# Converting float64 weights with 16-bit operations into a word of their own, in an attention and two-layer feed-forward kernel

## Chip, cores and metric

One NeuronCore of a Trainium2 chip runs the kernel. The metric is the device time of one execution in microseconds; the time before is the median of three runs.

## What is computed

The inputs are attention operands in float32 and the weights of two gated feed-forward layers in float64. Shapes: batch 4, 8 heads, 576 positions, head width 64; 2304 tokens of width 512; hidden width 1536.

```python
scores = q @ k.T / sqrt(64) + (cum[:, None] - cum[None, :])   # cum = cumsum(log(clip(f)))
attn   = softmax(causal(scores)) @ v                          # per batch and head
x      = attn as [2304, 512]
xn     = x / sqrt(mean(x*x) + 1e-6) * rms_g
y      = (silu(xn @ w_gate) * (xn @ w_val)) @ w_out           # first layer
z      = (silu(y @ w2_gate) * (y @ w2_val)) @ w2_out          # second layer, the output
```

Matrix products keep near-float32 accuracy: each operand is split into a rounded high part and a remainder, and three products of parts (high·high, high·low, low·high) are added up in PSUM.

## The kernel before

**Tokens and groups.** The tokens are worked on in four groups: three of 512 and a last one of 768. For each group the attention of its tokens comes first, then the norm, then the two layers. Attention work of a later group is put between the matmuls of an earlier one.

**Weights.** A layer has 36 weight tiles of 128 x 512 (24 for the gate and value products, 12 for the output product), so a group uses 72. The float64 values come from HBM only once, for group 0: `convert(i)` turns tile i into float32, stores it in HBM (`w_f`), and `split` makes the high and low parts (`whl`: a copy at L301, a subtraction at L306). Groups 1 and later fetch the float32 tiles or the split ones from HBM and convert nothing. In groups 0 to 2 one tile feeds four steps (`mm3`, L1700 to L1702) of three 512-column matmuls, so four L1702 matmuls stand for one tile used.

**Conversion.** One float64 is two 32-bit words. The tile lands in `x` (named `w`, from `w64_slots`: 4 buffers, one of them lent out at the start). Five operations follow:

- L1632 to L1636, the rebase: the high word, read as float32, times 2^-112, into `t`. On ACT (L1632), DVE (L1634) or POOL (L1636).
- L1642 (ACT) or L1644 (DVE), the low word's top three bits: byte 3 of each value is shifted right by 5 and written over byte 4, the lowest byte of the high word, in place. It has to wait for the rebase, which reads that word.
- L1648 (DVE): the high word with all but the sign and those three bits masked off, into `k` (`wk`, 2 buffers). After it `x` is free, and the load of a later tile (L1623) can be issued.
- L1654 (DVE): `t` shifted left by 3, joined with `k`. The result is the float32 tile.
- then the store (L1658) and `split`.

**Order of the work.** A planner written in Python runs when the program is built. Every operation is a request with one or more engines, a duration in us for each, and sometimes a handicap in us that is added to the end of that choice. The planner always takes the request that can start earliest by its model, ties going by priority, and puts it at the end of the chosen engine's queue. What it writes is a fixed order for each in-order engine; on the chip the engines wait by semaphores only. `DVL` stands for DVE operations that it doesn't let run beside a POOL operation. The handicaps are lists by phase (`HAND_LOW[plan.phase]`): phase 0 lasts until group 0 has used eight tiles, phase 1 until group 1 has, and so on. While group 0 has not used twelve tiles, the planner fills gaps of TensorE with matmuls whose result nobody uses (L372; L381 at the very start).

**Where the conversion meets other work.** In group 0 DVE and ACT also do the softmax (L672, L680, L700), the norm (sums at L966 to L972, a power on POOL at L1003, three small copies at L1008, the scaled rows at L1025, split into `X` at L301 and L306) and the gate (L1794, L1796, L1817).

Of the kernel before, what the change touches and what calls it, by code (L numbers as in the profile page):

```python
# [8 lines left out]
F32 = mybir.dt.float32  # L9
F32R = mybir.dt.float32r  # L10
I32 = mybir.dt.int32
U8 = mybir.dt.uint8
AF = mybir.ActivationFunctionType
ALU = mybir.AluOpType
AX = mybir.AxisListType
# [75 lines left out]
SP_START, SP_GATE = 1.55, 3  # L91
# [180 lines left out]
def tile_attention_moe_moe(  # L272
# [1334 lines left out]
    users = [1 + (i // FIRST == 1) for i in range(TOTAL)]  # L1607
    last_use = [0.0] * TOTAL

    def split(i, t, e):  # L1610
# [8 lines left out]
    def convert(i):  # L1619
        x, e0 = yield Take(w64_slots, (w_raw[i - 1],) * (i > 0) + (cum_here,) * (i == W_FREE))  # L1620
        later(w_raw[i], e0)
        src = (w1, w2)[i // NPIECE][i % NPIECE].bitcast(I32)
        el = yield op("SP", dma(P * WP * 8), lambda: nc.sync.dma_start(x.rearrange("p n t -> p (n t)"), src), e0)  # L1623
        t, e1 = yield Take(w32_slots, (el, w_t32[i - 1]) if i else (el,))
        later(w_t32[i], e1)
        k, e2 = yield Take(wk_slots, ())
        u8 = x.rearrange("p n t -> p (n t)").bitcast(U8).rearrange("p (n t) -> p n t", t=8)
        high = x[:, :, 1]

        et = yield either(  # L1630
            (("ACT", act(WP) + 0.06, 0.0), ("DVL", dve2(WP), HAND_CONV[plan.phase]), ("POOL", 0.7, HAND_CONV[plan.phase])),
            lambda e: nc.scalar.mul(t, high.bitcast(F32), 2.0**-112)  # L1632
            if e == "ACT"
            else nc.vector.tensor_scalar(t, high.bitcast(F32), 2.0**-112, None, op0=ALU.mult)  # L1634
            if e == "DVE"
            else nc.gpsimd.tensor_scalar(t, high.bitcast(F32), rebase, 1.0, op0=ALU.mult, op1=ALU.mult),  # L1636
            el, e1,
        )
# [12 lines left out]
        ti = t.bitcast(I32)  # L1651
        e = yield op(
            "DVL", dve(WP) + 0.035,
            lambda: nc.vector.scalar_tensor_tensor(ti, ti, 3, k, op0=ALU.logical_shift_left, op1=ALU.bitwise_or), e, et,  # L1654
        )
        wk_slots.give(k, e)
        later(w_split[i], e)
        es = yield op("SP", dma(P * WP * 4), lambda: nc.sync.dma_start(w_d[i], t), e)  # L1658
        later(stored[i], es)
        e = yield from split(i, t, e)  # L1660
        w32_slots.give(t, Event(max(e.t, es.t)))
# [32 lines left out]
            yield wait(w_raw[i])  # L1694


    def mm3(o, w, c, x, start, stop):
        (xh, xl), cs = (t[:, :NW] for t in x), slice(c * P, (c + 1) * P)
# [12 lines left out]
    def moe():  # L1711

        n = NW
        for g in range(NG):
            at = 0
            ready = [[x_ready[g][i][k] for i in range(2)] for k in range(KT)]
            for layer in range(2):
                base = (2 * g + layer) * NPIECE
                h_ready = [Event() for _ in range(MT)]
                if g == NG - 1:  # L1720
                    yield wait(w_raw[base - 1])
                    for r in range(MT // 2):
# [18 lines left out]
                for m in range(MT):  # L1741
                    pair = []
                    for j in range(2):
                        pc = base + 2 * m + j
                        bank, e0 = yield Take(banks, (w_ready[pc], *ready[0]))
                        for k in range(KT):
                            e = yield op(
                                "PE", 3 * pe(n),
                                lambda: mm3(bank, w_tiles[pc], k, XX[k], k == 0, k == KT - 1),
                                e0, w_ready[pc], *ready[k],  # L1750
                            )
                        used(pc, e)
                        later(steps[g][at], e)
                        at += 1
                        pair.append((bank, e))
                        if j == 0:
                            mid = Event()
                            half = []
                            spawn(gate(bank, e, half, mid), 0.0)
                        else:  # L1760
                            spawn(finish(pair, half, mid, HH[m], h_ready[m], H_PSUM[g](2 * m)), 0.0)
                    progress(g, at)
                if layer:
                    later(x_free[g + 1], e)
                y_ready = [Event() for _ in range(KT)]
                for d in range(KT):
                    bank, e0 = yield Take(banks, (h_ready[0],))
                    for j in range(3):
                        pc = base + 2 * MT + 3 * d + j
                        for c in range(4):  # L1770
                            m = 4 * j + c
                            e = yield op(
                                "PE", 3 * pe(n),
                                lambda: mm3(bank, w_tiles[pc], c, HH[m], m == 0, m == MT - 1),
                                e0, w_ready[pc], h_ready[m],
                            )
                        used(pc, e)
                        later(steps[g][at], e)
                        at += 1
                    spawn(evac(bank, e, layer, d, g, y_ready[d]), 0.1)  # L1780
                    progress(g, at)
                ready = [[y] for y in y_ready]
            if g == NG - 2:
                later(h_free, e)

    def progress(g, at):
# [4 lines left out]
    def gate(bank, e, half, mid):  # L1791
        n = NW
        th, e0 = yield Take(tmp_slots, ())
        e = yield op("ACT", actp(n), lambda: nc.scalar.activation(th, bank, AF.Tanh, scale=0.5), e, e0)  # L1794
        e = yield op(
            "DVE", dve(n), lambda: nc.vector.scalar_tensor_tensor(th, th, 1.0, bank, op0=ALU.add, op1=ALU.mult), e,  # L1796
        )
        banks.give(bank, e)
        half.append(th)
# [6 lines left out]
        half.append(th)  # L1806
        later(mid, e)

    def finish(pair, half, mid, hl, ready, psum):
        n = NW  # L1810
        bank, e = pair[1]
        yield wait(mid, e)
        th = half[0]
        hi, lo = hl
        o = bank if psum else th
        e = yield op(
            "DVE", dve(n), lambda: nc.vector.scalar_tensor_tensor(o, th, 0.5, bank, op0=ALU.mult, op1=ALU.mult), e, mid,  # L1817
        )
        if psum:
            tmp_slots.give(th, e)  # L1820
# [88 lines left out]
```

## Time and profile before

| | |
|---|---|
| runs | 1101.67, 1098.95, 1102.04 us; median 1101.67 us |
| the profiled execution | 1098.85 us, its span 1097.1 us (1.75 us lie around the span) |
| mean granted TensorE clock | 0.989 |
| busy in the span | PE 1078.0 us (98%), DVE 803.8 (73%), ACT 628.6 (57%), POOL 468.2 (43%) |
| moved by DMA | 282.21 MB, 257 GB/s in the mean |

PE is TensorE, PEld its weight load, DVE VectorE, ACT ScalarE, POOL GpSimd, SP SyncE, which issues the DMAs. Times in rows are us from the span's start, unless marked ns. A granted clock of 1.0 is 2.4 GHz, 0.5 is 1.2 GHz. "x41" counts instructions. Rows of one in-order engine can overlap a little: a row's duration runs from start to end, and the next one may start before that end. PE's busy time counts the unused fill matmuls too.

### The profile page before, as it was taken

Reading aid. Unit: us, or ns where it says so; the run is one execution under the profiler, and the core shown is the slowest. Engines: PE = TensorE matmul, PEld = TensorE weight load, DVE = VectorE, ACT = ScalarE, POOL = GpSimd, SP = SyncE. Lnnn points to the kernel's source line nnn. Section 1 sums busy time; section 2 is a strip of 40 time slices with the busy share of each in tenths; the row PEclk is TensorE's granted clock in tenths of the full one; section 3 lists DMA queues with packets and bytes.
Section 4 is the critical chain, followed back from the end, with each engine's and each line's share of the span. In section 5 each row is a group of like instructions: output and inputs, shape, how many; then the busy total and the mean of one; then the engine's idle time right before and its main releaser. Section 6 shows DMA issues by size and latency. Waiting matters only on the chain.

```text
span 1097.1 us, 17688 instructions
## 1 busy us (share of the span) xinstructions
PE 1078.0 (98%) x5547; PEld 949.6 (87%) x5547; DVE 803.8 (73%) x1709; ACT 628.6 (57%) x1409; POOL 468.2 (43%) x492
## 2 busy tenths in 40 slices
PE   8989999998999999999999999999999999999998
PEld 7968888886888888888888888888889999999998
DVE  5989888889556655866756776777767878788773
ACT  4967787886555765677525565456643334443352
POOL 2323211334156665666515585558732441233410
PEclk8989999998999999999999999999999999999999
DMA  7746679664799776776699999997996557754683
GB/s 211 221 160 223 226 262 317 223 228 142 267 383 374 255 247 234 251 251 237 242 345 377 332 341 346 355 343 276 336 332 203 168 188 243 240 171 173 198 261 106
DMA packets 136496, 282.21 MB, mean 257 GB/s; under 512 B 14674, under 2 KB 57490, under 8 KB 136402
## 3 DMA queue, kind: packets, MB, share of 16 engines
q1 hardware_dynamic: 136404, 281.10, 74.6%
q8 instruction: 44, 0.72, 0.3%
q14 instruction: 48, 0.39, 0.1%
HBM read 194.32 MB, written 86.65 MB: 256 GB/s over the span
## 4 chain that ended last, share of the span: by engine, by line
PE 90%; DVE 5%; DMA 2%; POOL 1%; issue 1%; ACT 0%; SPq 0%; POOLq 0%; ACTq 0%
PE bank L1700 18%; PE bank L1702 17%; PE bank L1701 17%; PE bank L1414 5%; PE bank L1416 5%; PE bank L1415 5%; PE bank L939 3%; PE bank L911 3%; PE bank L1324 3%; PE bank L1323 3%; PE bank L1322 3%; PE bank L802 2%; PE bank L803 2%; DMA w<-w 1%; PE bank L658 1%; PE bank L734 1%
## 5 line engine op out<-in xcount | busy, mean ns | idle before, releaser
L306 POOL TENSOR_TENSOR whl<-w,whl 128x512 fp32r<-128x512 f32 x126 | 167.2, 1330 | 216.9 <-ACT whl L301 178.2
L1700 PE MATMUL bank<-X,whl 128*128 128x512 f32 x564 | 227.5, 403 | 3.3 <-ACT X L301 3.3
L1702 PE MATMUL bank<-X,whl 128*128 128x512 f32 x564 | 221.0, 392 | 0.0
L1701 PE MATMUL bank<-X,whl 128*128 128x512 f32 x564 | 221.0, 392 | 0.0
L301 ACT CAST whl<-w 128x512 fp32r<-128x512 f32 x179 | 110.7, 622 | 47.8 <-PE bank L1701 17.7
L1700 PEld LDWEIGHTS bank<-X,whl 128*128 128x128 f32 x564 | 106.6, 189 | 23.8 <-ACT X L301 3.5
L1702 PEld LDWEIGHTS bank<-X,whl 128*128 128x128 f32 x564 | 106.3, 189 | 23.1
L1701 PEld LDWEIGHTS bank<-X,whl 128*128 128x128 f32 x564 | 106.6, 189 | 19.6 <-DVE X L306 0.4
L1700 PE MATMUL bank<-H,whl 128*128 128x512 f32 x215 | 87.4, 407 | 4.4 <-ACT whl L301 4.4
L1702 PE MATMUL bank<-H,whl 128*128 128x512 f32 x215 | 85.4, 397 | 0.2 <-DVE whl L306 0.2
L1701 PE MATMUL bank<-H,whl 128*128 128x512 f32 x215 | 85.2, 396 | 0.0
L1804 ACT ACTIVATE tmp<-bank 128x384 f32<-128x384 f32 x48 | 23.6, 491 | 90.8 <-DVE bank L1452 90.5
L1636 POOL TENSOR_SCALAR w<-w,rebase 128x512 f32<-128x512 f32 x24 | 24.8, 1038 | 106.1 <-PE bank L1702 42.2
L1794 ACT ACTIVATE tmp<-bank 128x512 f32<-128x512 f32 x72 | 43.3, 601 | 40.6 <-PE bank L1702 39.1
L1796 DVE SCALAR_TENSOR_TENSOR tmp<-tmp,bank 128x512 f32<-128x512 f32 x72 | 49.2, 684 | 22.7 <-ACT tmp L1794 22.0
L306 DVE TENSOR_TENSOR whl<-w,whl 128x512 fp32r<-128x512 f32 x71 | 49.5, 702 | 20.9 <-ACT whl L301 20.6
L820 DVE TENSOR_REDUCE tm<-bank 128x1 f32<-128x512 f32 (+1 forms) x96 | 50.4, 561 | 17.9 <-PE bank L803 9.1
L1817 DVE SCALAR_TENSOR_TENSOR bank<-tmp,bank 128x512 f32<-128x512 f32 x60 | 41.6, 694 | 26.6 <-PE bank L1702 25.9
L1642 ACT ACTIVATE w<-w,kbias 128x512 uint8<-128x512 uint8 x41 | 60.2, 1468 | 1.1 <-DVE w L1634 0.6
L923 DVE TENSOR_TENSOR pl<-bank,ph 128x512 fp32r<-128x512 f32 (+1 forms) x80 | 49.9, 632 | 11.3 <-ACT ph L301 10.5
L306 POOL TENSOR_TENSOR kb<-raw,k 64x576 fp32r<-64x576 f32 x31 | 44.3, 1429 | 20.2 <-ACT k L301 14.2
L1700 PEld LDWEIGHTS bank<-H,whl 128*128 128x128 f32 x215 | 40.6, 189 | 13.5 <-ACT whl L301 4.9
(296 smaller groups left out, 2900.4 us busy)
## 6 DMA issues: line engine op xcount, KB each, us to landing
whl<-w_split SPq DMA_DIRECT2D x90, 512.0 KB
w<-w SPq DMA_DIRECT2D x72, 512.0 KB
w<-w_f SPq DMA_DIRECT2D x144, 256.0 KB
w_split<-whl SPq DMA_DIRECT2D x72, 512.0 KB
w_f<-w SPq DMA_DIRECT2D x72, 256.0 KB
w_sums<-w SPq DMA_DIRECT2D x48, 256.0 KB
w_sums_split<-whl SPq DMA_DIRECT2D x23, 512.0 KB
w<-w_sums SPq DMA_DIRECT2D x41, 256.0 KB
```

Of the source, the lines that this page charges most:

```text
L301: nc.scalar.copy(o, i)
L306: (nc.vector if e == "DVE" else nc.gpsimd).tensor_tensor(o, a, b, op=ALU.subtract)
L820: em = yield op("DVE", dve(m), lambda: nc.vector.tensor_reduce(st[:, c + i : c + i + 1], bank[:, :m], axis=AX.X, op=ALU.max), e)
L923: e = yield op("DVE", dve(n), lambda: nc.vector.tensor_tensor(low, src, o.bitcast(F32), op=ALU.subtract), e)
L1414: nc.tensor.matmul(o, w[:, 0, cs], xh, start=c == 0, stop=False)
L1415: nc.tensor.matmul(o, w[:, 0, cs], xl, start=False, stop=False)
L1416: nc.tensor.matmul(o, w[:, 1, cs], xh, start=False, stop=c == 1)
L1642: lambda e: nc.scalar.activation(u8[:, :, 4], u8[:, :, 3], AF.Identity, scale=1.0 / 32, bias=kbias)
L1700: nc.tensor.matmul(o, wh[:, cs], xh, start=start, stop=False)
L1701: nc.tensor.matmul(o, wh[:, cs], xl, start=False, stop=False)
L1702: nc.tensor.matmul(o, wl[:, cs], xh, start=False, stop=stop)
L1796: "DVE", dve(n), lambda: nc.vector.scalar_tensor_tensor(th, th, 1.0, bank, op0=ALU.add, op1=ALU.mult), e,
```

## The change

The two operations on the high word in place give way to two that write 16-bit halves of `k`: the low word's top 16 bits shifted right by 13 go to the lower half of `k` (ACT or DVE), and the high word's top 16 bits, masked to the sign, go to its upper half (DVE). Neither touches `x`, so neither waits for the rebase any more; both wait for the load and for a free `k`. L1654 waits for all three. On ACT the shift is a scale of 1/8192 with a bias that makes rounding act as a floor. In the planner the durations become 0.65 us (ACT) and 0.447 us (DVE) for the low half, 0.447 us for the sign, and the rebase on POOL is put at 1.04 us in place of 0.7. `HAND_LOW` becomes 0.5 in phases 0 and 1 (before: -0.22 and 0).

The diff also brings a way of running the first hidden tiles of group 0 in halves (`halves`, `SPLIT_M`); `SPLIT_M` is 0, so none of it runs, and `mm3`, `gate` and `finish` get arguments that leave their instructions as they were.

```diff
-HAND_LOW = (-0.22, 0, 9, -0.01, 0.08)
+HAND_LOW = (0.5, 0.5, 9, -0.01, 0.08)
+A16, D16, S16 = 0.65, 0.447, 0.447
+SPLIT_M = 0
...
-    nc.gpsimd.memset(kbias, -15.5 / 32)
+    nc.gpsimd.memset(kbias, -4095.5 / 8192)
...
-        u8 = x.rearrange("p n t -> p (n t)").bitcast(U8).rearrange("p (n t) -> p n t", t=8)
+        x16 = x.rearrange("p n t -> p (n t)").bitcast(U16).rearrange("p (n t) -> p n t", t=4)
+        k16 = k.bitcast(U16).rearrange("p (n t) -> p n t", t=2)
...
-            (("ACT", act(WP) + 0.06, 0.0), ("DVL", dve2(WP), HAND_CONV[plan.phase]), ("POOL", 0.7, HAND_CONV[plan.phase])),
+            (("ACT", act(WP) + 0.06, 0.0), ("DVL", dve2(WP), HAND_CONV[plan.phase]), ("POOL", 1.04, HAND_CONV[plan.phase])),
...
-        e = yield either(
-            (("ACT", 1.465, 0.0), ("DVL", 0.762, HAND_LOW[plan.phase])),
-            lambda e: nc.scalar.activation(u8[:, :, 4], u8[:, :, 3], AF.Identity, scale=1.0 / 32, bias=kbias)
+        ek = yield either(
+            (("ACT", A16, 0.0), ("DVL", D16, HAND_LOW[plan.phase])),
+            lambda e: nc.scalar.activation(k16[:, :, 0], x16[:, :, 1], AF.Identity, scale=1.0 / 8192, bias=kbias)
             if e == "ACT"
-            else nc.vector.tensor_scalar(u8[:, :, 4], u8[:, :, 3], 5, None, op0=ALU.logical_shift_right),
-            et,
+            else nc.vector.tensor_scalar(k16[:, :, 0], x16[:, :, 1], 13, None, op0=ALU.logical_shift_right),
+            el, e2,
         )
-        e = yield op(
-            "DVL", dve2(WP), lambda: nc.vector.tensor_scalar(k, high, 7 - 2**31, None, op0=ALU.bitwise_and), e, e2
-        )
+        e = yield op("DVL", S16, lambda: nc.vector.tensor_scalar(k16[:, :, 1], x16[:, :, 3], 2**15, None, op0=ALU.bitwise_and), el, e2)
+        e = both(e, ek)
         w64_slots.give(x, Event(max(e.t, et.t)))
```

## Rows read from the trace of the kernel before

**Rows 1.** The page's 40 slices of the span: PE's busy tenths.

```profile
PE   8989999998999999999999999999999999999998
```

**Rows 2.** Stages of group 0 by windows: length, then busy us (instructions) of each engine, clock, DMA.

```profile
0.00:71.00 71.00, 60.73 (x377) 56.14 (x377) 57.22 (x174) 47.50 (x157) 21.15 (x30) 0.92 0.70 216
71.00:190.00 119.00, 118.92 (x537) 97.94 (x537) 102.28 (x199) 93.33 (x162) 21.77 (x18) 0.98 0.72 240
190.00:264.00 74.00, 74.00 (x347) 61.60 (x346) 63.22 (x124) 58.66 (x112) 25.58 (x23) 1.00 0.62 209
...
24.00:62.00 38.00, 37.56 (x265) 34.99 (x263) 36.49 (x114) 33.73 (x115) 12.42 (x11) 1.00 0.73 236
```

**Rows 3.** Waits of PE in 0 to 300 us: total, times, longest.

```profile
PE bank L1700 <- ACT X L301: 3.3, 1, 3.3
```

**Rows 4.** Timeline of PE around 264 us: start, duration, instruction.

```profile
263.78 0.40 PE L1701 MATMUL bank<-H,whl 128*128 128x512 f32 x1
264.01 0.40 PE L1702 MATMUL bank<-H,whl 128*128 128x512 f32 x1
268.82 0.79 PE L1700 MATMUL bank<-H,whl 128*128 128x512 f32 x1 [4.42 <-ACT whl L301]
...
274.36 0.40 PE L1700 MATMUL bank<-H,whl 128*128 128x512 f32 x1
```

**Rows 5.** Windows, the L1654 joins of DVE alone: length, busy us (instructions), clock, DMA.

```profile
0.00:71.00 71.00, 6.03 (x9) 0.92 0.70 216
71.00:190.00 119.00, 24.77 (x35) 0.98 0.72 240
190.00:264.00 74.00, 13.60 (x18) 1.00 0.62 209
```

**Rows 6.** Windows, the L1702 matmuls alone: PE busy, weight load busy.

```profile
71.00:190.00 119.00, 60.34 (x152) 28.97 (x152) 0.98 0.72 240
190.00:264.00 74.00, 37.12 (x95) 18.03 (x96) 1.00 0.62 209
```

**Rows 7.** Timeline of DVE, 257 to 267 us.

```profile
257.45 0.51 DVE L1008 COPY sm<-sm 32x8 f32<-32x8 f32 x3
...
261.68 5.31 DVE L1025 SCALAR_TENSOR_TENSOR tmp<-xT,gam,mb 128x256 f32<-128x256 f32 x6
266.91 1.21 DVE L1654 SCALAR_TENSOR_TENSOR w<-w,wk 128x512 int32<-128x512 int32 x1
```

**Rows 8.** Timeline of POOL at 261 us.

```profile
261.40 7.30 POOL L306 TENSOR_TENSOR X<-tmp,X 128x256 fp32r<-128x256 f32 x8 [2.25 <-ACT X L301]
```

**Rows 9.** The conversion's lines: ns min/median/max, first and last start.

```profile
L1642 ACT ACTIVATE w<-w,kbias x41: 1439/1467/1507, 52.2 to 286.2; 128x512 uint8<-128x512 uint8 x41
L1644 DVE TENSOR_SCALAR w<-w x31: 736/758/929, 17.1 to 284.6; 128x512 uint8<-128x512 uint8 x31
L1648 DVE TENSOR_SCALAR wk<-w x72: 384/422/1489, 19.3 to 287.7; 128x512 int32<-128x512 int32 x72
L1632 ACT ACTIVATE w<-w x31: 653/672/723, 98.5 to 285.5; 128x512 f32<-128x512 f32 x31
```

**Rows 10.** Timeline of DVE, 55 to 60 us: a byte shift, a mask, and what follows each.

```profile
55.64 0.76 DVE L1644 TENSOR_SCALAR w<-w 128x512 uint8<-128x512 uint8 x1
56.18 0.47 DVE L972 TENSOR_TENSOR acc<-acc,tmp 128x256 f32<-128x256 f32 x1
...
59.19 0.41 DVE L1648 TENSOR_SCALAR wk<-w 128x512 int32<-128x512 int32 x1
59.52 0.44 DVE L981 TRANSPOSE_TENSOR_REDUCE sm<-acc 128x8 f32<-128x256 f32 x1
```

**Rows 11.** Timeline of ACT, 222 to 224 us: a byte shift and what follows it.

```profile
222.60 1.46 ACT L1642 ACTIVATE w<-w,kbias 128x512 uint8<-128x512 uint8 x1
223.79 0.69 ACT L301 CAST H<-tmp 128x512 fp32r<-128x512 f32 x1
```

**Rows 12.** Timeline of DVE at 65 us: the norm's three copies.

```profile
65.33 3.75 DVE L1008 COPY sm<-sm 32x8 f32<-32x8 f32 x3 [0.34 <-POOL sm L1003]
```

More of the change, by code (lines that the diff above doesn't have):

```diff
@@ L11 @@
 I32 = mybir.dt.int32
-U8 = mybir.dt.uint8
+U16 = mybir.dt.uint16
 AF = mybir.ActivationFunctionType
@@ L1606, in tile_attention_moe_moe @@
     w_tiles = [None] * TOTAL
-    users = [1 + (i // FIRST == 1) for i in range(TOTAL)]
+    users = [1 + (i // FIRST == 1) + (i < 2 * SPLIT_M) for i in range(TOTAL)]
     last_use = [0.0] * TOTAL
@@ L1694, in weights, with mm3 @@
             yield wait(w_raw[i])
-    def mm3(o, w, c, x, start, stop):
-        (xh, xl), cs = (t[:, :NW] for t in x), slice(c * P, (c + 1) * P)
+    def mm3(o, w, c, x, start, stop, columns=slice(0, NW)):
+        (xh, xl), cs = (t[:, columns] for t in x), slice(c * P, (c + 1) * P)
         wh, wl = w[:, 0], w[:, 1]
@@ L1740, in moe @@
                     continue
-                for m in range(MT):
+                halved = SPLIT_M if g == layer == 0 else 0
+                if halved:
+                    for s in range(2):
+                        spawn(halves(s, steps[0], h_ready), 5 + 0.0005 * s)
+                    yield wait(*steps[0][: 2 * halved])
+                    at = 2 * halved
+                for m in range(halved, MT):
                     pair = []
@@ L1758, in moe @@
                             half = []
-                            spawn(gate(bank, e, half, mid), 0.0)
+                            spawn(gate(n, bank, e, half, mid), 0.0)
                         else:
-                            spawn(finish(pair, half, mid, HH[m], h_ready[m], H_PSUM[g](2 * m)), 0.0)
+                            spawn(finish(n, 0, pair, half, mid, HH[m], h_ready[m], H_PSUM[g](2 * m)), 0.0)
                     progress(g, at)
@@ L1784, in moe, with halves @@
                 later(h_free, e)
+    halves_ready = [[Event() for _ in range(2)] for _ in range(SPLIT_M)]
+    def halves(s, steps_, h_ready):
+        n = SPLIT
+        ready = [x_ready[0][s][k] for k in range(KT)]
+        for m in range(SPLIT_M):
+            pair = []
+            for j in range(2):
+                pc = 2 * m + j
+                bank, e0 = yield Take(banks, (w_ready[pc], ready[0]))
+                o = bank[:, :n]
+                for k in range(KT):
+                    e = yield op(
+                        "PE", 3 * pe(n),
+                        lambda: mm3(o, w_tiles[pc], k, XX[k], k == 0, k == KT - 1, slice(s * n, (s + 1) * n)),
+                        e0, w_ready[pc], ready[k],
+                    )
+                used(pc, e)
+                if s:
+                    later(steps_[pc], e)
+                pair.append((bank, e))
+                if j == 0:
+                    mid, half = Event(), []
+                    spawn(gate(n, bank, e, half, mid), 0.0)
+                else:
+                    spawn(finish(n, s * n, pair, half, mid, HH[m], halves_ready[m][s], H_PSUM[0](2 * m + s)), 0.0)
+        if s:
+            for m in range(SPLIT_M):
+                yield wait(*halves_ready[m])
+                later(h_ready[m], both(*halves_ready[m]))
     def progress(g, at):
@@ L1789, in progress, with gate @@
             plan.phase = max(plan.phase, g + 1)
-    def gate(bank, e, half, mid):
-        n = NW
+    def gate(n, bank, e, half, mid):
         th, e0 = yield Take(tmp_slots, ())
-        e = yield op("ACT", actp(n), lambda: nc.scalar.activation(th, bank, AF.Tanh, scale=0.5), e, e0)
+        a, b = th[:, :n], bank[:, :n]
+        e = yield op("ACT", actp(n), lambda: nc.scalar.activation(a, b, AF.Tanh, scale=0.5), e, e0)
         e = yield op(
-            "DVE", dve(n), lambda: nc.vector.scalar_tensor_tensor(th, th, 1.0, bank, op0=ALU.add, op1=ALU.mult), e,
+            "DVE", dve(n), lambda: nc.vector.scalar_tensor_tensor(a, a, 1.0, b, op0=ALU.add, op1=ALU.mult), e,
         )
@@ L1807, in gate_silu, with finish @@
         later(mid, e)
-    def finish(pair, half, mid, hl, ready, psum):
-        n = NW
+    def finish(n, at, pair, half, mid, hl, ready, psum):
         bank, e = pair[1]
@@ L1813, in finish @@
         th = half[0]
-        hi, lo = hl
-        o = bank if psum else th
+        hi, lo = (x[:, at : at + n] for x in hl)
+        a, b = th[:, :n], bank[:, :n]
+        o = b if psum else a
         e = yield op(
-            "DVE", dve(n), lambda: nc.vector.scalar_tensor_tensor(o, th, 0.5, bank, op0=ALU.mult, op1=ALU.mult), e, mid,
+            "DVE", dve(n), lambda: nc.vector.scalar_tensor_tensor(o, a, 0.5, b, op0=ALU.mult, op1=ALU.mult), e, mid,
         )
```

## The prediction

> **What bounds the kernel now.** I began with the page's slices [rows 1]: from the twelfth slice, some 302 us, PE's digit is 9 to the end, save the last. There TensorE is the bound, and conversion is over (its last start is at 287.7 us [rows 9]). So the change can act only before 300 us, and what it saves there is handed on to the end unless something later takes it back. The windows of group 0 come next [rows 2]. Up to 71 us PE looks busy, but partly with fill matmuls: the first matmul on the weights waits for `X`, the normed attention output, at the end of a 3.3 us stall [rows 3]. The engines that make it are nearly full: between 24 and 62 us DVE is busy 36.49 of 38 us and ACT 33.73 [rows 2]. From 71 to 264 us PE has no gap to speak of (118.92 of 119 and 74.00 of 74 us), with DVE at 86% and 85% [rows 2]. Then comes the one large stall: at 268.82 PE had waited 4.42 us for the high part of a weight tile (ACT, L301) [rows 4].
>
> That stall I read with two counts. By 71 us 9 tiles are joined, then 35 by 190, then 18 by 264, 62 in all [rows 5]. PE uses 152/4 = 38 tiles by 190 and 95/4 = 23.75 more by 264, 61.75 in all [rows 6]. The lead of the conversion over PE is 9 tiles at 71 us, 6 at 190, a quarter of a tile at 264: the buffer has run dry. What falls on the empty buffer is a burst: six norm operations take DVE 5.31 us, and the next join starts behind them at 266.91 [rows 7], while POOL runs eight subtractions without a break, 7.30 us [rows 8]. So conversion is late as a whole, and the burst shows it.
>
> **The change, part by part.** *The low word's bits.* Before, 41 on ACT at 1.467 us and 31 on DVE at 0.758 [rows 9]. What an operation takes from an in-order engine is start to start: 222.60 to 223.79, 1.19 us on ACT [rows 11]; 55.64 to 56.18, 0.54 us on DVE [rows 10]. No row has a 16-bit operation. The cheap bound is a 32-bit one: on DVE the mask L1648, median 0.422 us, start to start 59.19 to 59.52, 0.33 us [rows 9, 10]; on ACT L1632, 0.672 us, which reads the same 8-byte steps [rows 9], so 0.79 us less than the byte form. The dear bound is the byte form itself. I take the cheap end: the new operation reads one value per 8 bytes as L1632 and L1648 do, and writes a tile of its own, while the byte form writes single bytes into the words that it reads. The saving is 1.467 - 0.672 = 0.79 us for each one on ACT; on DVE 0.54 - 0.33 = 0.21 if it stays, and 0.54 if it goes to ACT, which then bears 0.67. The handicap of 0.5 sends it to ACT unless ACT is 0.3 us (0.5 + 0.447 - 0.65) later than DVE.
>
> The byte row bears on a rule. The Trainium skill, "VectorE: DVE Perf Modes", section "What auto-detection actually checks", lets a one-source operation between SBUF tiles use both ports, at two results a cycle, whatever its type, if the outermost counts are even. The byte shift's 758 ns against the mask's 422 for the same 512 elements [rows 9] contradicts it for bytes in place. By the rule the 16-bit form would take the mask's 422 ns and the sum below would stand; by the byte row the slower rival's would.
>
> *The sign.* It replaces the mask one for one, 72 times on DVE: 0.33 us before, the same after at the cheap end, 0.54 at the dear one. I take 0.
>
> *The waits.* Shift and mask no longer stand behind the rebase and each other, so `x` is free sooner by about one ACT byte shift (1.2 us), and loads start sooner. DMA has room for them (share 0.62 from 190 to 264 us [rows 2]). `k` is taken as before. No wait is added to a queue; the sign can wait for the load at the head of DVE's queue, with softmax behind it, as the rebase or the byte shift could.
>
> *The rebase on POOL at 1.04 us* in the planner pushes some of it to ACT and DVE. No row shows how many. Between none and half of the 18 conversions from 190 to 264 us, at 0.672 us on ACT, that is 0 to 6 us of engine time there; I take 2, since POOL is busy only 25.58 of 74 us [rows 2] and stays the free engine.
>
> *Two-port operations.* The Trainium skill, "SBUF — State Buffer", section "Who interferes with whom", says that a DVE operation in a two-port mode and a GpSimd one shut each other out for a whole instruction. It speaks against the change wherever a byte shift becomes such an operation. The rows agree in kind: the mask's longest is 1489 ns beside a median of 422, the byte shift's only 929 beside 758 [rows 9].
>
> *The sum.* (a) Up to 71 us nine tiles are joined. If all their shifts stay on DVE, 9 x 0.21 = 1.9 us; if all leave, 9 x 0.54 = 4.9 us of DVE, but with 6 us more on ACT, which has 4.3 us to spare between 24 and 62 us. I take 2.5 us, near the first: two full engines share a saving. (b) From 190 to 264 us PE uses a tile in 74/23.75 = 3.1 us. Covering 4.4 us needs 1.4 more tiles of lead, 19.4 conversions for 18, 8% more. If the 18 split like the 72, ten byte shifts are on ACT and eight on DVE: 10 x 0.79 + 8 x 0.21 = 9.6 us less work, minus 2 for the rebases, 7.6 us. A conversion with its split takes about 0.61 + 0.33 + 0.67 + 0.67 + 0.69 us beside the low word's share (join, mask, rebase, high part, low part, the last two priced like L1632 and the join), 3 us after the change, so 7.6 us are 2.5 tiles; the stretch before adds its own. That is over 1.4, and the stall should close: 4.42 us. With it goes the slow stretch behind it. From 268.82 to 274.36 PE issues 12 matmuls in 5.54 us; at the pace before it (263.78 to 264.01, 0.23 us) they take 2.8 [rows 4], so 2.7 us come back. The clock had been full up to 264 us (1.00 [rows 2]), and matmuls at 0.43 us in place of 0.23 after an idle stretch are the lower of the two levels, 1.2 GHz. Sum: 2.5 + 4.4 + 2.7 = 9.6 us. The profiled execution took 1098.85 us (1.75 of it around the span), so it would take 1089.3. It lies 2.8 us under the median of the runs shown, 1101.67, from which the same saving gives 1092.1. The forecast is for such a median: 1092 us.
>
> **The rivals.** *No change that shows.* The burst stays where it is, with DVE blocked for 5.31 us [rows 7], and the planner spends the freed time on attention instead of lead, since it takes what can start first. Then only (a) is left, and a part of that goes to ACT's queue: 1099 to 1102 us. For it: ten idle microseconds on DVE from 190 to 264 us [rows 2] already bring no lead. Against it: in that stretch each conversion lies behind a 1.2 us byte shift in ACT's queue.
>
> *Slower.* Sub-word writes cost what bytes cost. Then each sign takes 0.54 us for 0.33, and the shift saves nothing. Up to 71 us that is 9 x 0.21 = 1.9 us on a full DVE, and from 71 to 264 us 53 x 0.21 = 11.1 us on a DVE with 27.5 us idle; if half of it hits conversion while the lead is already gone at 264, 5.6 us are added to the stall: 1101.7 + 7.5 = 1109 us. It decides from a sign operation of about 0.6 us up. The byte rows speak for it; that the new target shares no word with the source speaks against it.
>
> *A new stall.* The planner's order changes everywhere. One burst that lands on an empty buffer elsewhere costs what the one at 264 us costs, 7.1 us: with (a) and (b) gained, 1099 us; two of them, 1106.
>
> *More.* Around 65 us three small copies of the norm take 3.75 us [rows 12] where they need 0.51 [rows 7], behind POOL work; this delays `X`, and the PE stall before 71 us [rows 3] has its own slow stretch. With fewer rebases on POOL, 3.2 us come back and some 2.7 of slow clock: 1092 - 5.9 = 1086, and 1084 with (a) at its upper end.
>
> **How the numbers follow.** Chances: the forecast 0.52; more 0.14; no change 0.17; slower by dear 16-bit operations 0.09; a new stall 0.08. The likeliest gives 1092 us. The range takes in the rival with more (1084, less 1 for scatter) and no change, and one new stall: 1083 to 1103. Outside stay two stalls and the dear 16-bit operations, together under 2 in 10. A difference of 0.3%, 3.3 us, is about what the runs can tell from none (the three spread over 3.1 us). Faster by more than that: 0.52 and 0.14, about 0.66. Within: 0.17 and a little of a single new stall, 0.19. Slower: 0.09 and the rest, 0.15.
>
> **What would show it.** The new operations in the groups by line: ACT about 0.67 us, DVE about 0.42, both without a wait for the rebase. PE's first weight matmul before 69 us. In the waits of PE no row for `whl` over 1 us, and in the counts a lead of two tiles or more when the eight subtractions of `X` run. The prediction is wrong if the 16-bit rows read over 0.6 us on DVE or over 1.2 us on ACT, if the stall on `whl` stays at 4 us, or if new waits of PE appear after 300 us.

## The result and the profile after

The kernel after takes 1090.53 us (median of 6 runs, 1086.23 to 1092.51), the kernel before 1101.10 us in the same series (6 runs, 1098.95 to 1102.04). The ratio is 0.9901, 95% interval [0.9878, 0.9924]: faster by about 10.6 us. The profiled execution took 1089.15 us (span 1087.4), so against the 1098.85 us of the one before it gains 9.7 us. The forecast was 1092 us, and 1089.3 us for a profiled execution.

The lines of the new code lie a little lower in the file: the shift is L1645 (ACT) and L1647 (DVE), the sign L1650, the join L1656, the rebase L1635, L1637 and L1639, the three weight matmuls L1702 to L1704, the split L303 and L308, the norm's copies L1010.

The page's busy times and slices of the kernel after answer to [rows 1]. PE's digit is 9 between the first slice and the last, so the 8 that the kernel before has in the tenth slice is gone, and the granted clock has one digit under 9, the first:

```profile
PE 1074.0 (99%) x5542; PEld 947.7 (87%) x5542; DVE 793.0 (73%) x1695; ACT 618.6 (57%) x1428; POOL 460.7 (42%) x487
...
PE   8999999999999999999999999999999999999998
...
PEclk8999999999999999999999999999999999999999
```

PE was busy 1078.0 us before. The span is 9.7 us shorter: 4.0 us less busy time and 5.7 us less idle time. The gain lies before 300 us: PE is idle 8.33 us there where it was 14.94. After 300 us the kernel after even waits 1.1 us where the kernel before waits 0.4.

The stages by windows answer to [rows 2]; columns as there:

```profile
0.00:71.00 71.00, 62.67 (x375) 57.76 (x376) 55.51 (x186) 51.28 (x166) 13.33 (x23) 0.90 0.66 201
...
71.00:190.00 119.00, 119.00 (x553) 98.77 (x552) 98.41 (x193) 89.80 (x176) 22.79 (x20) 1.00 0.79 263
190.00:264.00 74.00, 74.00 (x345) 61.32 (x344) 64.07 (x123) 61.44 (x125) 22.58 (x22) 1.00 0.73 247
264.00:300.00 36.00, 36.00 (x157) 29.27 (x156) 18.74 (x31) 17.32 (x32) 13.89 (x22) 1.00 0.77 269
```

From 264 to 300 us PE is now busy all the time at full clock. All of PE's waits, the counterpart to [rows 3] and to the stall in [rows 4] (line, releaser: total us, times, longest):

```profile
PE bank L383 <- DVE H L370: 3.3, 1, 3.3
PE bank L721 <- ACT d L702: 2.6, 2, 2.2
PE bank L660 <- DMA qk<-cum: 1.8, 1, 1.8
PE bank L913 <- POOL dB L863: 0.6, 1, 0.6
PE bank L721 <- DVE d L704: 0.5, 1, 0.5
PE bank L913 <- ACT dA L861: 0.5, 1, 0.5
```

No row is left for `whl`, nor for `X`. In place of the wait on `X` stands one of 2.2 us on `d`, an attention tile from ACT, some 8 us earlier. PE's timeline there, start, duration, instruction, and the idle time before it:

```profile
63.51 0.33 PE L721 MATMUL bank<-mi,d 128*128 128x128 f32 x1 [2.20 <-ACT d L702]
...
69.28 0.40 PE L1702 MATMUL bank<-X,whl 128*128 128x512 f32 x1
```

The first matmul on the weights starts at 69.28 us, 1.8 us earlier than before (71.08, behind the stall of [rows 3]), and takes 0.40 us, so the clock is already full. Windows of PE alone show where the clock was low, first before (length, PE busy, clock, DMA), then after:

```profile
65.00:71.00 6.00, 1.54 (x12) 0.85 0.47 144
71.00:76.00 5.00, 4.92 (x13) 0.50 0.16 61
...
264.00:276.00 12.00, 7.41 (x22) 0.72 0.52 162
```

```profile
65.00:71.00 6.00, 5.91 (x26) 0.72 0.12 34
71.00:76.00 5.00, 5.00 (x26) 1.00 0.93 273
...
264.00:276.00 12.00, 12.00 (x53) 1.00 0.41 131
```

Before, the matmuls from 71 to 76 us ran at 0.50 (1.2 GHz) behind the idle stretch, 10 of them on weights and 3 short ones; the kernel after does 26 there, 8 of them of 256 columns. After, the low stretch falls on attention matmuls before 69 us and is shorter: in clock time it costs 6.00 x (1 - 0.72) = 1.7 us where the old one cost 5.00 x (1 - 0.50) = 2.5. The one behind the stall at 264 us is gone.

The two counts that the prediction used, joins of DVE and then the third weight matmul of PE, answer to [rows 5, 6]:

```profile
0.00:71.00 71.00, 6.21 (x9) 0.90 0.66 201
71.00:190.00 119.00, 25.66 (x38) 1.00 0.79 263
190.00:264.00 74.00, 15.84 (x22) 1.00 0.73 247
```

```profile
0.00:71.00 71.00, 0.78 (x2) 0.47 (x3) 0.90 0.66 201
71.00:190.00 119.00, 60.23 (x154) 28.86 (x154) 1.00 0.79 263
190.00:264.00 74.00, 37.91 (x98) 18.23 (x97) 1.00 0.73 247
```

A matmul that runs across the edge of two windows stands in both; the window from 0 to 264 us alone has 253 of them. So by 264 us 9 + 38 + 22 = 69 tiles are joined and 253/4 = 63.25 used: the lead is 5.75 tiles, where it was a quarter of a tile. PE has also used 253 - 247 = 6 quarters of a tile more.

The conversion's lines answer to [rows 9] (ns min/median/max, first and last start):

```profile
L1645 ACT ACTIVATE wk<-w,kbias x59: 862/886/902, 58.2 to 274.0; 128x512 uint16<-128x512 uint16 x59
L1647 DVE TENSOR_SCALAR wk<-w x13: 425/455/478, 16.7 to 252.5; 128x512 uint16<-128x512 uint16 x13
L1650 DVE TENSOR_SCALAR wk<-w x72: 419/459/1574, 17.1 to 272.6; 128x512 uint16<-128x512 uint16 x72
L1635 ACT ACTIVATE w<-w x41: 635/667/691, 80.5 to 272.9; 128x512 f32<-128x512 f32 x41
```

On DVE the 16-bit forms cost what the prediction took (0.455 and 0.459 for 0.42). On ACT the shift takes 0.886 us, neither the 0.672 that was taken nor the 1.467 of the byte form.

### The profile page after: what moved, and what is told of

Same layout as the page of the kernel before. It is cut to its first block, busy times and chain, and to the rows that moved or that the text cites. A ratio compares the mean times of both kernels' runs of the same rounds, so it can differ in the third digit from the quotient of the medians.

```text
span 1087.4 us, 17697 instructions
## 1 busy us (share of the span) xinstructions
PE 1074.0 (99%) x5542; PEld 947.7 (87%) x5542; DVE 793.0 (73%) x1695; ACT 618.6 (57%) x1428; POOL 460.7 (42%) x487
## 4 chain that ended last, share of the span: by engine, by line
PE 92%; DMA 3%; DVE 2%; ACT 1%; POOL 1%; issue 1%; SPq 0%; ACTq 0%; POOLq 0%
PE bank L1702 18%; PE bank L1703 17%; PE bank L1704 17%; PE bank L1416 5%; PE bank L1418 5%; PE bank L1417 5%; PE bank L941 3%; PE bank L913 3%; PE bank L1326 3%; PE bank L1325 3%; PE bank L1324 3%; PE bank L804 2%; PE bank L805 2%; PE bank L660 2%; PE bank L736 2%; DMA w<-w_f 1%
## 5 line engine op out<-in xcount | busy, mean ns | idle before, releaser
L308 POOL TENSOR_TENSOR whl<-w,whl 128x512 fp32r<-128x512 f32 x126 | 167.1, 1329 | 241.2 <-ACT whl L303 204.2
L1702 PE MATMUL bank<-X,whl 128*128 128x512 f32 x564 | 226.8, 402 | 0.0
L1704 PE MATMUL bank<-X,whl 128*128 128x512 f32 x564 | 220.6, 391 | 0.0
L303 ACT CAST whl<-w 128x512 fp32r<-128x512 f32 x178 | 108.8, 616 | 51.1 <-PE bank L1703 13.9
L1704 PEld LDWEIGHTS bank<-X,whl 128*128 128x128 f32 x564 | 106.0, 188 | 23.0
L1702 PEld LDWEIGHTS bank<-X,whl 128*128 128x128 f32 x564 | 106.3, 188 | 20.2
L1702 PE MATMUL bank<-H,whl 128*128 128x512 f32 x215 | 87.0, 405 | 0.0
L1704 PE MATMUL bank<-H,whl 128*128 128x512 f32 x215 | 85.1, 396 | 0.0
L308 DVE TENSOR_TENSOR whl<-w,whl 128x512 fp32r<-128x512 f32 x71 | 49.1, 699 | 19.3 <-ACT whl L303 18.3
L308 POOL TENSOR_TENSOR kb<-raw,k 64x576 fp32r<-64x576 f32 x32 | 45.7, 1429 | 21.0 <-ACT k L303 18.8
L1645 ACT ACTIVATE wk<-w,kbias 128x512 uint16<-128x512 uint16 x59 | 51.3, 885 | 2.3 <-DMA w<-w 1.9
L1417 PE MATMUL bank<-X,whl 128*128 128x384 f32 x154 | 51.5, 335 | 0.0
L1418 PE MATMUL bank<-X,whl 128*128 128x384 f32 x154 | 51.5, 335 | 0.0
```

The source lines that it names most:

```text
L303: nc.scalar.copy(o, i)
L308: (nc.vector if e == "DVE" else nc.gpsimd).tensor_tensor(o, a, b, op=ALU.subtract)
L1417: nc.tensor.matmul(o, w[:, 0, cs], xl, start=False, stop=False)
L1418: nc.tensor.matmul(o, w[:, 1, cs], xh, start=False, stop=c == 1)
L1645: lambda e: nc.scalar.activation(k16[:, :, 0], x16[:, :, 1], AF.Identity, scale=1.0 / 8192, bias=kbias)
```

## The experiments

Three theories stood at the start. **A**: the shift's time on the chip, on ACT and DVE, is what conversion lacked. **B**: the waits that were taken away did it. **C**: the planner's order did it, through the new prices and handicaps. And beside them a question: is it the 16 bits that are cheap, or the word of their own? There were three series, each with its own runs of the kernel before: 1100.34 us (21 runs) beside the constants, the waits kept and the byte in its own word; 1101.16 (16) beside the shift issued twice, the cheap prices for the byte, the measured prices and the old constants; 1100.17 (23) beside the price between, the own word only and the burst moved.

**Constants alone.** The kernel before with the changed handicaps and the rebase's price:

```diff
-HAND_LOW = (-0.22, 0, 9, -0.01, 0.08)
+HAND_LOW = (0.5, 0.5, 9, -0.01, 0.08)
...
-("POOL", 0.7, HAND_CONV[plan.phase])
+("POOL", 1.04, HAND_CONV[plan.phase])
```

> The kernel before with nothing but the planner's new constants: the handicap of 0.5 in phases 0 and 1 and 1.04 us for a rebase on POOL; the byte operations stay. Theory A (the gain is engine time that the cheaper operations free): about the time before, 1101 us, or slower, since the handicap sends 1.47 us byte shifts to ACT. Theory B (the gain is the waits on the rebase taken away): the same, about 1101. Theory C (the gain is a luckier order, from the constants): about 1091, and no stall of PE on a weight tile near 264 us.

1103.35 us (12 runs), ratio 1.0024 [1.0011, 1.0037]. The stall is still there and longer; PE's waits:

```profile
PE bank L1700 <- ACT whl L301: 6.1, 1, 6.1
...
PE bank L1702 <- POOL whl L306: 2.2, 1, 2.2
```

The constants bring nothing without the new operations.

**The waits kept.** The kernel after, but the shift also waits for the rebase (`et`), and the sign for the shift:

```diff
-            el, e2,
+            el, e2, et,
...
-... 2**15, None, op0=ALU.bitwise_and), el, e2)
+... 2**15, None, op0=ALU.bitwise_and), ek)
```

> The changed kernel with the old waits put back: the 16-bit shift waits for the rebase, the sign waits for the shift. Durations as in the changed kernel. Theory A (engine time): 1091 to 1094, no stall on a weight tile above 1 us. Theory B (waits): the gain goes, 1098 or more, with a stall on a weight tile of some us before 300 us. Theory C (order): anywhere, as the order is written anew.

1088.53 us (6 runs), ratio 0.9896 [0.9871, 0.9922]: all of the gain, and no wait on `whl`. Theory B falls. The earlier loads that the prediction listed under the waits are worth nothing that can be measured.

**A byte in a word of its own.** The kernel after, with the shift on bytes again, written to the lowest byte of `k` (whose other bytes are zeroed once) and priced as before:

```diff
-A16, D16, S16 = 0.65, 0.447, 0.447
+A16, D16, S16 = 1.465, 0.762, 0.447
...
-nc.scalar.activation(k16[:, :, 0], x16[:, :, 1], AF.Identity, scale=1.0 / 8192, bias=kbias)
+nc.scalar.activation(k8[:, :, 0], x8[:, :, 3], AF.Identity, scale=1.0 / 32, bias=kbias)
```

> The changed kernel with the low word's shift as a byte operation that writes the lowest byte of k (k is zeroed at the start), with no wait on the rebase; the planner is given the byte durations, 1.465 and 0.762 us. Theory A: if the byte form in its own word still takes 1.47 us on ACT and 0.76 on DVE, the gain goes, 1097 to 1102 us. Theory B: 1091 to 1093 all the same. If the byte form in its own word takes about 0.9 us on ACT, what was dear was the write in place, and both theories give some 1092.

1109.08 us (10 runs), ratio 1.0069 [1.0047, 1.0091], and yet the byte operation is as cheap as the 16-bit one. Its group by line, and PE's longest wait:

```profile
L1650 ACT ACTIVATE wk<-w,kbias 128x512 uint8<-128x512 uint8 x48 | 42.4, 883 | 3.5 <-DVE w L1661 1.8 <-DMA w<-w 1.4 <-ACT whl L304 0.2
```

```profile
PE bank L1709 <- DVE whl L309: 8.8, 1, 8.8
```

Cheap operations with dear prices give an order that loses 9 us: besides that wait, fill matmuls take 13.60 us of PE from 71 to 130 us (0.52 before). That a time belongs to the operation and a loss to the plan had to be told apart next.

**The operations by themselves.** A kernel of these operations alone runs each form four times, 512 elements on each of 128 partitions.

> No part of the reference is computed: one weight tile is loaded and each form of the shift and of a 32-bit operation runs four times in a row on DVE and on ACT; the output is filler. If a write of less than a word is what costs, the byte in place, the byte in its own word and the 16-bit forms are all dear on ACT (0.9 to 1.5 us) and the strided 32-bit write is not (0.67 us). If the step of the write costs, the 16-bit form with an 8-byte step takes 1.47 us like the byte one, the 16-bit form packed without gaps takes 0.67 us, and the strided 32-bit write is dear too. If the byte type costs, both byte forms take 1.47 us on ACT and 0.76 on DVE, and all 16-bit forms 0.9 and 0.46.

Groups of ACT and of DVE (busy us, mean ns). `x` names writes at an 8-byte step into the tile that is read, `k` writes at a 4-byte step, `c` packed ones:

```profile
L64 ACT ACTIVATE xA<-xA,bias 128x512 uint8<-128x512 uint8 x4 | 5.7, 1437 | 0.1
L70 ACT ACTIVATE xA<-xA,bias 128x512 uint16<-128x512 uint16 x4 | 5.7, 1420 | 0.1
L68 ACT ACTIVATE kA<-xA,bias 128x512 uint16<-128x512 uint16 x4 | 3.5, 874 | 0.1
L66 ACT ACTIVATE kA<-xA,bias 128x512 uint8<-128x512 uint8 x4 | 3.4, 861 | 0.1
L76 ACT ACTIVATE kA<-xA,bias 128x512 f32<-128x512 f32 x4 | 3.0, 750 | 0.1
...
L74 ACT ACTIVATE kA<-xA 128x512 f32<-128x512 f32 x4 | 2.6, 654 | 0.1
```

```profile
L44 DVE TENSOR_SCALAR xD<-xD 128x512 uint16<-128x512 uint16 x4 | 2.9, 735 | 0.1
...
L44 DVE TENSOR_SCALAR kD<-xD 128x512 uint16<-128x512 uint16 x4 | 1.8, 456 | 0.1
...
L59 DVE TENSOR_SCALAR xD<-xD 128x512 int32<-128x512 int32 x4 | 1.7, 426 | 0.1
```

Byte or 16 bits makes no difference (within 3%); where the result goes does. The last two rows are whole words, with a bias operand as the shift has it and without one. A second kernel of that kind separates the step from writing in place: `y` and `b` are other tiles written at an 8-byte step, `kA<-kA` is in place at a 4-byte step.

> Computes no part of the reference: conversion's operations by themselves, 512 elements for each of 128 partitions, four of each. It separates what the first probe left together. If the step of the written elements sets the price, 16-bit and byte results at an 8-byte step into another tile take about 1.42 us on ACT and 0.73 on DVE, and 16-bit results at a 4-byte step in place about 0.87 and 0.46. If writing into the tile that is read sets it, the first pair falls to 0.87 and 0.46 and the second rises to 1.42 and 0.73. Packed bytes and packed 16-bit words at 0.73 and 0.43, a whole word as result on ACT at 0.75, and 32-bit results at an 8-byte step at 0.65 and 0.43, if only writes of part of a word cost.

```profile
L76 ACT ACTIVATE b<-xA,bias 128x512 uint8<-128x512 uint8 x4 | 5.8, 1442 | 0.1
L72 ACT ACTIVATE b<-xA,bias 128x512 uint16<-128x512 uint16 x4 | 5.8, 1438 | 0.1
...
L72 ACT ACTIVATE kA<-kA,bias 128x512 uint16<-128x512 uint16 x4 | 3.4, 850 | 0.1
L72 ACT ACTIVATE kA<-xA,bias 128x512 int32<-128x512 uint16 x4 | 3.0, 751 | 0.1
...
L72 ACT ACTIVATE cA<-cA,bias 128x512 uint16<-128x512 uint16 x4 | 2.9, 721 | 0.1
L86 ACT ACTIVATE b<-xA 128x512 f32<-128x512 f32 x4 | 2.6, 648 | 0.1
```

```profile
L49 DVE TENSOR_SCALAR y<-xD x8: 734/738/1017, 4.1 to 10.0; 128x512 uint16<-128x512 uint16 x4, 128x512 uint8<-128x512 uint8 x4
L49 DVE TENSOR_SCALAR kD<-kD x4: 453/454/485, 10.6 to 12.1; 128x512 uint16<-128x512 uint16 x4
```

```profile
L49 DVE TENSOR_SCALAR cD<-cD 128x512 uint16<-128x512 uint16 x4 | 1.2, 294 | 0.1
```

The step of the written elements sets the price, for results of less than a word: 1.44 us at 8 bytes, 0.85 at 4, 0.72 packed on ACT; 0.74, 0.45 and 0.43 on DVE. In place or not, it is the same within 3%. A whole word pays nothing for the 8-byte step (0.648 us against 0.654 on ACT without a bias, 0.427 against 0.426 on DVE). The last row goes from packed to packed: there the source counts too, 0.294 us on DVE against 0.436 where it is read at an 8-byte step.

**The shift issued twice.** The order and the plan of the kernel after, unchanged on every engine; only each shift runs twice, at 0.884 us each:

```diff
+        def low(e, k16, x16):
+            for _ in range(2):
+                if e == "ACT":
...
-            lambda e: nc.scalar.activation(k16[:, :, 0], x16[:, :, 1], ...
+            lambda e: low(e, k16, x16),
```

> The changed kernel, order and planner costs untouched, but every 16-bit shift is issued twice in a row, so that on the chip it takes about what the byte form took (ACT some 1.6 us for 1.47, DVE some 0.8 for 0.76). Theory A (engine time on the chip): the gain goes, 1098 us or more, and PE waits some us for a weight tile before 300 us. Theory C (the order that the planner writes): most of the gain stays, 1094 us or less.

1109.27 us (6 runs), ratio 1.0076 [1.0059, 1.0092], 18.7 us over the median of the kernel after. ACT is busy 72.60 of the 74 us from 190 to 264 us, and PE waits for it:

```profile
PE bank L721 <- ACT d L702: 10.2, 9, 3.3
PE bank L1707 <- ACT X L1880: 4.0, 1, 4.0
```

So the chip's time for the shift matters in this order (theory A). The test is a harsh one: 59 shifts at twice 0.884 us are 103.3 us of ACT, where the 41 byte shifts of the kernel before were 60.2; how much of the 18.7 us a shift at the byte's own 1.467 us would cost isn't shown. What runs late is not `whl`: with a dear shift in this order the attention's tiles behind it on ACT are late.

**The byte, with the cheap prices.** As the byte kernel above, but priced 0.65, 0.447 and 0.447, so that the order is the one of the kernel after on every engine, save two memsets on POOL:

> The run before with the byte shift into its own word, but the planner is given the costs of the changed kernel (0.65 and 0.447 us), which makes the order on every engine that of the changed kernel. If the bytes as such cost nothing and the dear plan was what made that run slow: 1089 to 1092 us, as the changed kernel. If the byte form has a cost that its rows don't show: over 1097.

1088.99 us (6 runs), ratio 0.989 [0.987, 0.991]. Bytes cost nothing here. The 9 us lost with the same operations at the dear prices were the plan's.

**The measured prices.** The kernel after, with the planner told what its trace shows:

```diff
-A16, D16, S16 = 0.65, 0.447, 0.447
+A16, D16, S16 = 0.886, 0.457, 0.457
```

> The changed kernel with the durations that its own profile shows given to the planner: 0.886 us on ACT, 0.457 on DVE. Theory C with the reading that a true plan is a better one: 1085 to 1089. Theory A, in which only the chip's durations count: 1089 to 1093. If orders differ by chance: anywhere between 1086 and 1098.

1102.36 us (12 runs), ratio 1.0013 [1.0001, 1.0025]: the gain is gone, with the same operations. No wait on `whl` comes back, and the lead at 264 us is 69 joined against 238/4 = 59.5 used. What is lost lies at the start: PE waits there, its first weight matmul comes at 75.06 us, and fill matmuls take 7.78 us from 71 to 130 us (1.47 in the kernel after).

```profile
65.48 0.33 PE L721 MATMUL bank<-mi,d 128*128 128x128 f32 x1 [3.37 <-ACT d L702]
```

By 264 us PE is 253 - 238 = 15 quarters of a tile behind the kernel after. A quarter is three matmuls of 0.23 us, so 10.4 us; the two spans differ by 11.0.

**A price between.**

```diff
-A16, D16, S16 = 0.65, 0.447, 0.447
+A16, D16, S16 = 0.75, 0.447, 0.447
```

> The kernel after with one planner price changed: the shift on ACT told as 0.75 us in place of 0.65 (told 0.886, with DVE's two at 0.457, the time was 1102). If the price moves the time smoothly, by its own size, 0.1 of 0.236 us gives 1090 + 5 = 1095 us. If each plan is a draw of its own, with the loss in the order of the start, anything from 1088 to 1104 us, and the time goes with the first weight matmul (69 us in the kernel after, 75 with the price of 0.886) and with fill matmuls between 71 and 130 us. If 0.65 was safely inside a flat stretch, 1089 to 1091 us.

1096.42 us (12 runs, 1092.99 to 1100.92), ratio 0.9968 [0.9951, 0.9985]: between the other two and near the smooth reading's 1095, though three points don't make a law. Its profiled execution is its fastest, so what the slower ones lose isn't seen.

**The old constants.** The kernel after with `HAND_LOW` and the rebase's 0.7 us of the kernel before.

> The changed kernel with the old handicaps (-0.22 and 0 in phases 0 and 1) and 0.7 us for a rebase on POOL. If the constants carry part of the gain: 1094 to 1099 us. If the operations carry it: 1089 to 1093.

1088.23 us (4 runs), ratio 0.9882 [0.9867, 0.9897]. The handicap of 0.5 and the rebase's price aren't needed.

**The own word only.** The kernel before with its handicaps, its rebase price, its byte shift and its waits; changed are the target of the shift (so it also waits for a free `k`, whose other bytes are zeroed once), the sign's 16-bit half and the three prices.

```diff
-nc.scalar.activation(u8[:, :, 4], u8[:, :, 3], ...)
+nc.scalar.activation(k8[:, :, 0], x8[:, :, 3], ...)
...
-nc.vector.tensor_scalar(k, high, 7 - 2**31, None, op0=ALU.bitwise_and)
+nc.vector.tensor_scalar(k16[:, :, 1], x16[:, :, 3], 2**15, None, op0=ALU.bitwise_and)
```

> The kernel before, with its own handicaps, its own price for the rebase on POOL, its byte operations and its waits (rebase, shift, then mask) all kept; changed are only that the shifted byte goes into a word of its own (the sign, a 16-bit operation, into the upper half of the same word) and the prices that the planner is told for the three operations. If the own word on the chip and its low price in the plan are the whole change, 1086 to 1091 us and no wait on whl over 1 us, as in the kernel after. If the parts left out matter together though each alone did not, 1094 to 1100 us.

1091.03 us (6 runs), ratio 0.9903 [0.988, 0.9927], no wait on `whl`. That is the whole gain. Here the first weight matmul starts at 72.43 us, later than in the kernel before, so an early first weight matmul is not what makes it.

**The burst moved.** The kernel before, with the low parts of group 1's `X` on DVE in place of POOL:

```diff
-        e = yield lo_op(n, lo, xn[:, :n], hi, e)
+        e = yield lo_op(n, lo, xn[:, :n], hi, e, hand=-9 if g == 1 else None)
```

> The kernel before with one thing changed: the low parts of X of group 1 (the run of eight subtractions on POOL that stood in front of the 4.4 us stall of TensorE at 264 us) are sent to DVE. Nothing of the conversion is changed, so its lead over TensorE at 264 us stays near zero. If the burst on POOL made the stall, it goes or falls below 1.5 us: 1094 to 1097 us. If the lack of lead made it (the prediction's reading), whoever does the subtractions, the stall stays at 3 us or more, on DVE's or ACT's part of the tile: 1099 to 1104 us.

1098.73 us (12 runs), ratio 0.9978 [0.9959, 0.9996]. The subtractions now run on DVE, in pieces between the scaled rows, and the stall stays, nearly as long and with slow matmuls behind it (0.79 us for the first):

```profile
269.09 0.79 PE L1700 MATMUL bank<-H,whl 128*128 128x512 f32 x1 [3.64 <-ACT whl L301]
```

By 264 us 62 tiles are joined and 246/4 = 61.5 used, a lead of half a tile. So it isn't POOL's subtractions that make the stall. But the burst is moved and not gone: on DVE no join starts from 256.39 to 267.44 us (255.36 to 266.91 in the kernel before). Two of the kernels above tell more, by starts of joins and of third weight matmuls. With the waits kept no join starts for 12.4 us from 250.4 us, with the old constants for 12.5 us from 253.4: longer than in the kernel before, and no wait on `whl` follows. At 250 us their leads are 64 - 234/4 = 5.5 and 66 - 234/4 = 7.5 tiles, where the kernel before has 61 - 227/4 = 4.25 and this one 60 - 226/4 = 3.5. What parts the kernels that stall there from those that don't is the lead with which they enter that stretch.

**Taken together** (medians in us, each kernel beside its own series of the kernel before; in the row of the dearer shift stand the byte in place, 1.467 us, and, told 0.65, the shift twice, 1.77 us):

| | planner told 0.65 | told more |
|---|---|---|
| shift of 0.89 us on ACT | 1090.5; 1088.5, 1089.0, 1088.2, 1091.0 with parts undone | 1096.4 (0.75), 1102.4 (0.886), 1109.1 (1.465) |
| dearer shift on ACT | 1109.3 | 1101 before, 1103.4 (1.465) |

As far as these kernels go, the gain needs both, a cheaper shift on the chip and a low price in the plan; no run has the byte in place told 0.65. It isn't one lucky order: the waits kept, the old constants and the own word only each have another order on all four compute engines than the kernel after, and all four orders made with 0.65 gain with the cheaper shift. The variants at 1088 and 1089 us aren't shown to be faster than the kernel after: the intervals of their ratios overlap with its own.

## Why the prediction held

**The mechanism, (b) and (c).** Conversion was late as a whole, and the stall at 264 us was its sign: this step was right. It asked for 19.4 conversions from 190 to 264 us; there were 22. The 4.42 us are gone, and so is the slow stretch behind them. The other kernels bear out the lead: stretches without a join as long as the one before do no harm where the lead is 5.5 tiles or more at 250 us.

How the conversions came to be more was foreseen only in part. The sum freed 0.79 us of ACT for each byte shift and 7.6 us in all from 190 to 264 us. There ACT's shifts and rebases now take 18.83 + 9.31 = 28.1 us for 22 conversions, where they took 19.12 + 4.03 = 23.2 for 18 joins and 19 shifts: 1.28 us for each conversion now and 1.2 to 1.3 then, so nothing was saved. DVE's share (rebase, shift, sign or mask) is 0.82 + 0.46 + 10.81 = 12.1 us, before 2.10 + 4.52 + 9.26 = 15.9: some 0.3 us less for each conversion, 6 to 7 us in 22. That is near the size of the sum, but on the other engine, and it met the size by luck.

**(a), up to 71 us.** 2.5 us were taken. PE is idle 8.33 us up to 71 us where it was 10.27, 1.9 us less, and the low clock costs 1.7 us in place of 2.5: together 2.7 us, the size that was taken. That the freed engine time of the sum brought it isn't shown. Part of the rival with more gain came true here: the norm's three copies take 1.65 us, from 63.81 us, where they took 3.75, `X` is no longer waited for, and the slow stretch behind that wait is gone. A new wait on `d` (2.2 us) and a low clock from 66 to 69 us took part of it back. An early first weight matmul isn't needed for the gain either: the kernel with the own word only has it 1.4 us later than before. So the sum of 9.6 us met 9.7 with (b) and (c) as reckoned (PE's idle time from 264 to 300 us went from 4.6 us to none) and with an (a) that was right in size and in part by luck.

**The price of the shift.** This is the term that was mis-sized: "I take the cheap end" held on DVE and not on ACT. Measured, 0.886 us, it saves 1.467 - 0.886 = 0.58 us for each, not 0.79. The planner, told 0.65, sent 59 shifts to ACT, not 41. In all, shifts and sign (before: mask) cost ACT 51.3 us where they cost 60.2, and DVE 33.8 + 5.9 = 39.7 us where they cost 23.1 + 33.6 = 56.7 (busy times of their groups). The saving came out on DVE more than on ACT.

**The reason given for the price** was half right. "Reads one value per 8 bytes as L1632 does, and writes a tile of its own" pointed to the target, and the target it was. But a tile of its own isn't the point: at an 8-byte step it costs the same 1.44 us. The step between written parts of words is. And the row that set the cheap end, L1632, has no bias operand: in the kernel of the operations alone whole words take 0.654 us without one and 0.750 with one, and the 16-bit result at a 4-byte step 0.874. So the shift lies over the cheap end by about 0.10 us for the form with the bias and 0.12 us for the part of a word.

**The waits** were given a gain in loads that the runs don't show. **The rebase**: POOL does 15 of them where it did 24, ACT 41 where it did 31. From 190 to 264 us that is 9.31 - 4.03 = 5.3 us more on ACT for the 2 us that were taken, near the upper end of its 0 to 6. With the old price the gain is the same.

**The signs.** Met: no row for `whl`, a lead over two tiles, no rebase in front of the shift, DVE's rows. Missed: ACT's 0.67 us, and a first weight matmul before 69 us, by 0.28 us. Of the signs of being wrong one came true in small: PE's waits after 300 us are 1.1 us, 0.5 of them on a tile that it didn't wait for before (`dA`).

**The rivals.** No change that shows: it would have had the stall stay, as it did with the constants alone. Dear 16-bit operations: the doubled shift gave 1109 us, the time that the prediction had for them, though by attention tiles late on ACT and not by the stall on `whl` that it reckoned with. A new stall: none in the kernel after, but the orders made with the measured prices show how near it was.

**Two-port operations.** The sign's longest, 1574 ns beside a median of 459, starts at 230.00 us, while a subtraction of POOL runs from 229.93 for 1.32 us. It agrees in kind, as the mask's did [rows 9], with the Trainium skill, "SBUF — State Buffer", section "Who interferes with whom". No run here shows what that costs the kernel.

**What stays open.** The prediction treated the planner's prices as part of the change's cost and not as a cause of their own. They are one: with the same operations, the byte in its own word, the plan alone moves the time from 1089 to 1109 us. Why a true price makes a worse start, and which choice of the planner does it, stays open.

## What to carry to other kernels

Where a buffer's lead has run dry, count what is made and what is used by stage; the burst that falls on the empty buffer is where it shows, and here moving it to another engine gained little (1.4 us), while with more lead a stretch as long did no harm. When the results of an operation are less than a word, give them to neighbouring addresses or write whole words, and time that form by itself before choosing a type. In a kernel whose order is written by a planner, change an operation and its price in separate runs: one can hide what the other does.

## What the runs showed of the hardware

Writes of part of a word with gaps between them are dear, whether bytes or 16 bits, for 512 elements on each partition: on ACT, with a bias operand, 1.42 to 1.44 us at an 8-byte step, 0.85 to 0.89 at 4, 0.72 to 0.75 packed or as whole words; on DVE 0.74, 0.45 and 0.43. Whole words at the 8-byte step cost no more than packed ones, 0.427 us against 0.426 on DVE. The Trainium skill, "VectorE: DVE Perf Modes", section "What auto-detection actually checks", makes the two-port mode depend on operands and counts, not on the width of a strided result. Parts of words at an 8-byte step take 0.735 us here against 0.426 for whole ones; whether the mode isn't taken there or doesn't reach its rate, no run tells apart. The Trainium skill, "Vector Engine (DVE) Microarchitecture Reference", section "5.2 Measured stream behaviour on trn2 (trn3 not measured)", says that a port has its full rate only for runs of two or more adjacent words; the whole words at an 8-byte step against packed ones, 0.427 and 0.426 us, don't show that price on the written side. Nearly all of these operations read at an 8-byte step. Where the reads alone were changed it made little difference: 16-bit results at a 4-byte step on ACT take 0.850 us read at 4 bytes and 0.874 at 8, and single copies of whole words on DVE 0.419 us read packed and 0.428 at 8 bytes. Packed 16-bit results on DVE are the exception, 0.294 us read packed and 0.436 at 8 bytes.
